# Streamed weight blocks of a recurrent attention layer, copied in DRAM so that a partition's three blocks lie together and are read in longer runs

## Chip, cores and metric

One core of a Trainium2 chip runs the whole kernel in one launch. The metric is the device time of a run in microseconds (us); runs shown here are of the same kernel and input, and the profile is one more execution with the hardware profiler on.

## Reference

Four layers are applied in turn, A, B, A, B, each added to its input. Both A layers use the same weights. The change lies in layer A, whose heart is a recurrence over 64 segments of 32 rows with 8 memory rows ahead of them:

```python
for s in range(n_seg):                       # 2048 / 32 = 64
    xs = x[:, s * seg_len:(s + 1) * seg_len, :]
    h = concatenate([mem, xs], axis=1)       # 8 + 32 rows of 640
    q, k, v = (einsum('btd,dhe->bhte', h, W) for W in (Wq, Wk, Wv))   # 32 heads of 192
    p = softmax(where(mask, einsum('bhqe,bhke->bhqk', q, k) * scale, -1e9))
    o = einsum('bhqk,bhke->bhqe', p, v)
    o = einsum('bhte,hed->btd', o, Wo)       # back to 640
    mem = o[:, :M, :]                        # the next segment waits for this
    outs.append(o[:, M:, :])
```

Layer B is a linear attention over all rows at once; the change does not touch it.

## The kernel before, in words

Each A layer has a part ahead of the recurrence (`A_pre`), which projects the last 8 rows of every segment, and the recurrence itself (`A_chain`). In the chain the 32 heads are worked off in four rounds of eight heads; even segments take the rounds in the order 0, 1, 2, 3 and odd ones in the order 3, 2, 1, 0. A round needs its columns of Wq, Wk and Wv: five blocks each (the 640 input rows are five blocks of 128 partitions) of 1536 bf16 columns, 3072 bytes a partition. The arena in SBUF holds most of these blocks for good (`res`). Three blocks of each matrix, of rounds 0 and 3 alone, share nine slots (`slot`, `SLOTS`), and the 12 row blocks of Wo of rounds 0 and 3 share one buffer (`wo_end`). So in every segment one of the two rounds is overwritten by the other: 9 blocks of 384 KB and 1920 KB of Wo, 5.4 MB, are streamed from DRAM per segment.

The order is written out by hand. In the first round of a segment (`n == 0`) `project` (L988) goes through the blocks with the slots first, and as soon as a slot's block has been multiplied, `load_slot` (L681) issues on SyncE (SP) the load of the same block for the last round of this segment; Q and V blocks in one transfer of 384 KB, K blocks in two of 192 KB, that is in runs of 3072 and 1536 bytes. After the second round's scores, `wo_round` (L1067) multiplies the first round's output with `wo_end`, and `load_wo` (L698) issues six transfers of 320 KB (runs of 2560 bytes out of `wo_rows`, a copy of Wo's rows laid out partition by partition). That makes 18 transfers per segment on SP's queue. The last round reads the Q blocks, the K blocks, the V blocks and at the segment's end all of `wo_end`; then the new memory rows go through VectorE (L1229, L1230) into the next segment's input `hT`, for which its first matmul waits.

GpSimd issues the smaller transfers: `kqb<-kqb` (L959) and `Vp<-vb` (L971) bring the memory rows' parts of Q, K and V for a later round, `otb<-otb` (L1058) stores a tile that has two buffers and is written again by ScalarE (L1053) or VectorE (L1051, L1054), and `Vp<-xn` (L939) brings the next segment's rows. `normalise` (L1115) on VectorE makes the weights `E` for which `attend` (L1038) waits.

`fill` and `SEG_FILL` (L1087) issue weight loads that compute nothing, a few per segment, and `keep_busy` matmuls that compute nothing.

Of the kernel before, what the change touches and what calls it, by code (L numbers as in the profile page):

```python
# [8 lines left out]
P = 128  # L9
BF16 = mybir.dt.bfloat16  # L10
# [7 lines left out]
SLOTS = {"Q": 3, "K": 3, "V": 3}  # L18
# [97 lines left out]
class Kernel:  # L116
# [526 lines left out]
    def layer_A(self, xn_dram, at_dram, li, x_raw=None):  # L643
        nc, tc = self.nc, self.tc
        KC, NSEG = self.KC, self.NSEG
        dram = self.dram
        NR = 4
        PW = 1536
        self.kqb_d = dram.tile([NR, P, NSEG, 192], BF16, name=f"kqb{li}")
        self.vb_d = dram.tile([NSEG, NR, 2, 8, 896], BF16, name=f"vb{li}")  # L650
        self.otb_d = dram.tile([P, NSEG, 384], BF16, name=f"otb{li}")
        wview = self.wview
        wov = self.A_Wo.rearrange("h d m -> (h d) m").rearrange("(c p) m -> p c m", p=P)
        low = self.view(0, LATE)
        at = LATE
        res, slot = {}, {}
        for r in (3, 2):
            for m in "KQV":
                for b in range(KC - (SLOTS[m] if r == 3 else 0)):
                    res[m, r, b] = low[:, len(res) * PW:len(res) * PW + PW]  # L660
        assert len(res) * PW * 2 == LATE
        for m, r, b in [(m, 0, b) for m in "KQV" for b in range(KC - SLOTS[m])] + \
                [(m, None, b) for m in "KQV" for b in range(KC - SLOTS[m], KC)] + [(m, 1, b) for m in "KQV" for b in range(KC)]:
            v = self.view(at, 2 * PW)
            at += 2 * PW
            if r is None:
                slot[m, b] = v
            else:
                res[m, r, b] = v
        holds = {}  # L670
        wo_mid = self.view(at, 24 * 1280)
        wo_end = self.view(at + 24 * 1280, 12 * 1280)
        assert at + 36 * 1280 == ARENA
        unread = set(res)

        def load_slot(m, r, b, whole=False):
            if holds.get((m, b)) != r:
                holds[m, b] = r
                w = PW if whole or m in "QV" else PW // 2
                for h in range(0, PW, w):  # L680
                    nc.sync.dma_start(out=slot[m, b][:, h:h + w], in_=wview[m][:, b, PW * r + h:PW * r + h + w])  # L681

        def load_matrix(m, r):
            for b in range(KC):
                if (m, r, b) in unread:
                    unread.remove((m, r, b))
                    nc.sync.dma_start(out=res[m, r, b], in_=wview[m][:, b, PW * r:PW * r + PW])
                elif (m, r, b) not in res:
                    load_slot(m, r, b, True)

        early = {(0, 4), (0, 5), (2, 4), (2, 5), (1, 0), (1, 1), (1, 2), (1, 3)}

        def load_wo(r, into=None, part=range(6)):
            t = into if into is not None else wo_end[:, :] if r in (0, 3) else wo_mid[:, 7680 * (r - 1):7680 * r]
            for k in part:
                tk = t[:, 1280 * k:1280 * k + 1280]
                if r in (0, 3):
                    self.last_load = nc.sync.dma_start(out=tk, in_=self.wo_rows[r // 3, :, 1280 * k:1280 * k + 1280])  # L698
                else:
                    nc.sync.dma_start(out=tk.rearrange("p (c m) -> p c m", m=640),  # L700
                                      in_=wov[:, 12 * r + 2 * k:12 * r + 2 * k + 2, :])

        def piece(m, r, b):
            assert (m, r, b) in res or holds[m, b] == r
            return res[m, r, b] if (m, r, b) in res else slot[m, b]

        if li == 0:
            self.wo_rows = dram.tile([2, P, 7680], BF16, name="wo_rows")

        def lay_out_wo(i):  # L710
            nc.sync.dma_start(out=self.wo_rows[i].rearrange("p (c m) -> p c m", m=640), in_=wov[:, 36 * i:36 * i + 12, :])

        def early_wo():
            for r in (2, 0, 1):
                load_wo(r, part=[k for k in range(6) if (r, k) in early])

        def late_wo(r, part=range(6)):
            load_wo(r, part=[k for k in part if (r, k) not in early])

        self.A_pre(xn_dram, li, load_matrix, piece, wo_mid, wo_end, lay_out_wo, early_wo, x_raw)  # L720
        self.A_chain(xn_dram, at_dram, li, load_slot, piece, load_wo, late_wo, wo_mid, wo_end, low)
        self.post_args = at_dram, wo_mid, wo_end, low

    def two_heads(self, ap):
# [188 lines left out]
        if x_raw is None:  # L913
            self.small.close()

    def A_chain(self, xn_dram, at_dram, li, load_slot, piece, load_wo, late_wo, wo_mid, wo_end, low):
        nc, tc, KC, NSEG = self.nc, self.tc, self.KC, self.NSEG
        scale = float(self.Dh) ** -0.5
        NR = 4
        with tc.tile_pool(name=f"A{li}_ch", reuse_waits="tile", bufs=1) as sp, \  # L920
# [17 lines left out]
            def load_rows(s):  # L938
                nc.gpsimd.dma_start(out=xr[8:32, :], in_=xn_dram[32 * s:32 * s + 24, :])  # L939

            def hx_transpose(hT, gs):
                for g in gs:
                    nc.vector.transpose(out=hT[32 * g:32 * g + 32, :, :],
                                        in_=xr[:, 160 * g:160 * g + 160].rearrange("p (j b) -> p b j", b=KC))
# [89 lines left out]
            def attend(E, n, OT=None):  # L1034
                O = [pop.tile([P, 512], F32, name=f"ps_o{x}", tag=f"o{x}") for x in range(2)]
                for x in range(2):
                    for k, e, i in ((0, 0, 0), (320, 1, 2), (128, 0, 1), (192, 1, 1)):
                        nc.tensor.matmul(O[x][:, 80 * i:80 * i + 80], lhsT=Vs[n % 2][0:80, 448 * x + k:448 * x + k + 128],  # L1038
                                         rhs=E[0:80, 160 * x + 80 * e:160 * x + 80 * e + 80], start=(k == 0),
                                         stop=(k == 192), skip_group_check=True)  # L1040
                if OT is None:
                    OT = sp.tile([P, 6, 64], BF16, name="OT", tag="OT")
                o = [x[:, 0:240].rearrange("p (i q) -> p i q", q=80) for x in O]
                nc.scalar.activation(out=OT[:, 0:3, :], in_=o[0][:, :, 0:64], func=ACT.Copy)  # L1044
                nc.vector.tensor_copy(out=OT[:, 3:6, :], in_=o[1][:, :, 0:64])
                return OT, o
# [80 lines left out]
            hT = new_hT()  # L1127
            hx_transpose(hT, range(4))
            load_rows(1)
            for s in range(NSEG):  # L1130
                W = pop.tile([P, 512], F32, name="ps_w", tag="w")
                order = rounds(s)
# [4 lines left out]
                def q_or_k(m, n):  # L1137
                    ps = pqp.tile([P, 512], F32, name="ps_qk", tag="qk")
                    project(hT, ps, m, n, s, range(KC))
                    return to_raw(ps, "OT" if m == "K" and n == 0 else "raw")  # L1140
# [4 lines left out]
                def tails_after(n):  # L1145
                    if n + 2 < NR:
                        extra_v(s, n + 2)
                    elif s + 1 < NSEG:
                        extra_v(s + 1, n + 2 - NR)
# [15 lines left out]
                for n in range(L):  # L1165
                    raw = q_or_k("Q", n + 1)
                    if n > 0:
                        OT, o = attend(Ep, n - 1)
                        tails_after(n - 1)
                    S, E = weigh(False)  # L1170
                    to_rows(raw, "Q")
                    if n > 0:
                        otb = keep_tail(o)
                    next_kq(s, n)
                    if n > 0:
                        store_tail(otb, s, order[n - 1])
                    to_rows(q_or_k("K", n + 1), "K")
                    sums(S, E)
                    normalise(S, E)
                    if n == 1:  # L1180
                        wo_round(W, order[n - 1], OT, True, False)
                        if n == 1:
                            if s < NSEG - 1:
                                load_wo(order[L])
                            else:
                                tails = [self.fetch_tails(tb, low) for tb in range(2)]
                    if n + 1 < L:
                        pv = v_banks()
                        project(hT, pv, "V", n + 1, s, range(KC))
                        v_rows(pv, n + 1)  # L1190
                    Ep = E
# [122 lines left out]
```

## Time and profile before

| what | value |
|---|---|
| runs | 3577.23, 3579.53, 3584.39 us; median 3579.53 us |
| the profiled execution's own time | 3596.84 us |
| its span, first to last instruction | 3595.1 us |
| granted TensorE clock, mean | 0.992 |
| PE busy | 3303.2 us (92%) |
| the two chains | about 205.9 to 1515.4 us and 2008.0 to 3318.6 us, 1309.5 and 1310.6 us |
| DMA share in the two chains | 0.83 and 0.83, at 287 and 286 GB/s |

PE is TensorE's matmuls, PEld its weight loads, DVE VectorE, ACT ScalarE, POOL GpSimd, SP SyncE. A wait is a stretch in which an engine stood idle, put down to what ended it; "issue" is a stretch that nothing in the profile's semaphores explains. "DMA share" is the mean busy share of the core's 16 DMA engines. Queue q1 is SP's, q0 GpSimd's, q8 TensorE's instructions.

### The profile page before, as it was taken

The numbers are of one execution on the slowest core, as the hardware profiler recorded it, in microseconds if no ns is written. First come the engines' busy times: TensorE is split into PE (matmuls) and PEld (weight loads), VectorE is DVE, ScalarE is ACT, GpSimd is POOL, SyncE is SP. The second block draws the span as 40 slices with busy tenths as digits, with TensorE's granted clock in tenths as the row PEclk, the third lists the DMA queues.
The fourth block names the chain that finished last, engine by engine and source line by source line (L and its number), as shares of the span: only waits on it lengthen the run. The fifth ranks groups of instructions, "written<-read, shape, count | busy, mean of one in ns | idle before, by whom it ended". The sixth has DMA issues, their size and how long they took to land.

```text
span 3595.1 us, 168452 instructions
## 1 busy us (share of the span) xinstructions
PE 3303.2 (92%) x70978; PEld 2275.7 (63%) x71391; DVE 2332.6 (65%) x6320; ACT 2034.5 (57%) x5233; POOL 1588.9 (44%) x4173
## 2 busy tenths in 40 slices
PE   9989999999999989989999889999999999999899
PEld 7756666666666666655377566666666666666553
DVE  5456666667667766746643566766676666776465
ACT  3356666666666656646432556666666666666463
POOL 3345555555555555530123455555555555555400
PEclk9999999999999999999999999999999999999999
DMA  8888888888888878860476888888888888888600
GB/s 319 325 289 279 287 294 284 277 290 296 282 284 293 296 272 283 297 217 1 145 275 216 289 273 276 292 283 292 274 296 287 290 279 290 299 278 287 221 1 30
DMA packets 452689, 929.38 MB, mean 259 GB/s; under 512 B 75338, under 2 KB 218330, under 8 KB 448858
## 3 DMA queue, kind: packets, MB, share of 16 engines
q1 hardware_dynamic: 382266, 817.56, 64.6%
q0 software_dynamic: 67744, 87.80, 8.0%
q8 instruction: 557, 9.13, 1.0%
q10 hardware_dynamic: 1920, 13.24, 0.9%
q14 instruction: 202, 1.65, 0.1%
HBM read 848.50 MB, written 73.73 MB: 257 GB/s over the span
## 4 chain that ended last, share of the span: by engine, by line
PE 47%; DMA 29%; DVE 9%; issue 6%; ACT 5%; POOL 1%; PEld 1%; SPq 1%; ACTq 0%; DVEq 0%; POOLq 0%
DMA arena<-wo_rows 18%; PE ps_qk L988 14%; PE ps_v L988 5%; DMA arena<-in_A_Wv_dram 5%; PE ps_pre L878 5%; PE ps_w L1067 4%; PE ps_o L1038 3%; PE ps_s L1030 3%; PE ps_pre L902 2%; DVE E L1115 2%; ACT raw L998 2%; DMA Vp<-vb 2%; PE kv L1269 2%; DVE QT L1006 1%; PE ps_s L1025 1%
## 5 line engine op out<-in xcount | busy, mean ns | idle before, releaser
L988 PEld LDWEIGHTS <-hT 128*32 128x32 bf16 x30720 | 874.4, 97 | 418.8 <-DVE hT L1230 53.9
L988 PE MATMUL ps_qk<-arena,hT 128*32 128x384 bf16 x20480 | 1031.0, 327 | 64.0 <-DVE hT L1230 55.8
L998 ACT ACTIVATE raw<-ps_qk 128x384 bf16<-128x384 f32 x1024 | 501.9, 490 | 366.1 <-DVE QT L1008 249.9
L988 PE MATMUL ps_v<-arena,hT 128*32 128x384 bf16 x10240 | 601.7, 327 | 22.8 <-DMA arena<-in_A_Wv_dram 22.3
L1067 PE MATMUL ps_w<-arena,OT 128*32 128x160 bf16 x18432 | 488.3, 234 | 46.4 <-DMA arena<-wo_rows 37.3
L971 POOL DMA_DIRECT2D Vp<-vb x512 | 258.3, 505 | 594.3 <-PE ps_o L1038 561.7
L1067 PEld LDWEIGHTS <-OT 128*32 128x32 bf16 x18432 | 391.0, 96 | 123.4 <-issue 53.8
L1003 DVE STREAM_TRANSPOSE KT<-raw 128x384 bf16<-128x384 bf16 x512 | 296.2, 578 | 195.4 <-ACT raw L998 191.5
L1006 DVE STREAM_TRANSPOSE QT<-raw 128x256 bf16<-128x256 bf16 x512 | 227.9, 445 | 238.5 <-ACT raw L998 196.2
L959 POOL DMA_DIRECT2D kqb<-kqb x512 | 290.9, 568 | 168.6 <-POOL KT L967 147.3
L1058 POOL DMA_DIRECT2D otb<-otb x512 | 282.8, 552 | 149.2 <-DVE otb L1054 117.0
L1019 DVE CAST Vp<-ps_v 64x384 bf16<-64x384 f32 x512 | 286.1, 559 | 85.8 <-ACT Vp L1017 74.5
L1115 DVE TENSOR_TENSOR E<-E,ps_s 80x320 bf16<-80x320 bf16 x512 | 247.4, 483 | 118.0 <-ACT ps_s L1114 117.1
L1017 ACT ACTIVATE Vp<-ps_v 64x384 bf16<-64x384 f32 x512 | 245.2, 479 | 107.6 <-PE ps_v L988 107.2
L1038 PEld LDWEIGHTS <-Vp 80*128 80x128 bf16 x4096 | 193.5, 99 | 175.2 <-issue 140.3
L1038 PE MATMUL ps_o<-E,Vp 80*128 80x80 bf16 x4096 | 233.1, 201 | 71.7 <-DVE E L1115 45.9
L1092 ACT ACTIVATE E<-ps_s 80x320 bf16<-80x320 f32 x512 | 221.4, 432 | 73.2 <-PE ps_s L1030 35.8
L951 ACT ACTIVATE Vp<-ps_w 32x160 bf16<-32x160 f32 x512 | 150.3, 294 | 157.9 <-DVE wt L1229 144.7
L964 POOL COPY QT<-kqb 128x64 bf16<-128x64 bf16 x512 | 124.4, 243 | 255.8 <-PE ps_s L1030 249.4
L1030 PE MATMUL ps_s<-QT,KT 128*80 128x80 bf16 (+1 forms) x3072 | 233.2, 213 | 2.7 <-POOL KT L967 2.6
L1044 ACT ACTIVATE OT<-ps_o 128x192 bf16<-128x192 f32 x384 | 126.1, 328 | 192.8 <-PE ps_o L1038 177.7
L1113 ACT ACTIVATE ps_s<-ps_s 80x320 f32<-80x320 f32 x512 | 214.7, 419 | 26.9 <-PE ps_s L1108 26.9
(158 smaller groups left out, 5362.3 us busy)
## 6 DMA issues: line engine op xcount, KB each, us to landing
arena<-wo_rows SPq DMA_DIRECT2D x780, 320.0 KB, 7.1
arena<-in_A_Wq_dram SPq DMA_DIRECT2D x427, 384.0 KB, 4.6
arena<-in_A_Wv_dram SPq DMA_DIRECT2D x427, 384.0 KB, 6.5
arena<-in_A_Wk_dram SPq DMA_DIRECT2D x768, 192.0 KB, 4.8
kqb<-kqb POOLq DMA_DIRECT2D x512, 48.0 KB, 5.3
arena<-in_A_Wk_dram SPq DMA_DIRECT2D x43, 384.0 KB, 7.7
vb<-arena POOLq DMA_DIRECT2D x128, 112.0 KB, 6.4
Vp<-vb POOLq DMA_DIRECT2D x512, 28.0 KB, 4.8
```

What stands on the lines that cost most here:

```text
L959: nc.gpsimd.dma_start(out=kqb[:], in_=self.kqb_d[r, :, s, :])
L971: nc.gpsimd.dma_start(out=Vs[n % 2][64:80, :], in_=self.vb_d[s, r].rearrange("g t f -> (g t) f"))
L988: nc.tensor.matmul(o[32 * g:32 * g + 32, 0:384], lhsT=hT[:, b, :], rhs=rhs, start=(i == 0), stop=(i == KC - 1), tile_position=(0, 32 * g), ...
L998: nc.scalar.activation(out=raw[:], in_=ps[:, 0:384], func=ACT.Copy)
L1003: nc.vector.transpose(out=KT[:, :, 0:64], in_=raw[:, :].rearrange("p (c j) -> p c j", j=64))
L1006: nc.vector.transpose(out=QT[:, :, 0:4:3, 0:64], in_=rv[:, :, 0:3:2, :])
L1019: nc.vector.tensor_copy(out=o, in_=i)
L1030: nc.tensor.matmul(S[0:80, c0:c0 + 80 * (q1 - q0)], lhsT=KT[:, 3 * x + i, :], rhs=QT[:, x, q0:q1, :], start=False, stop=(x == 1 and i == 2 ...
L1038: nc.tensor.matmul(O[x][:, 80 * i:80 * i + 80], lhsT=Vs[n % 2][0:80, 448 * x + k:448 * x + k + 128], rhs=E[0:80, 160 * x + 80 * e:160 * x ...
L1058: nc.gpsimd.dma_start(out=self.otb_d[:, s, 96 * r:96 * r + 96], in_=otb[:, :, :].rearrange("p c t -> p (c t)"))
L1067: nc.tensor.matmul(W[32 * g:32 * g + 32, 0:160], lhsT=OT[:, c, q:q + 32], rhs=w[:, 640 * i + 160 * g:640 * i + 160 * g + 160], start=(firs ...
L1115: nc.vector.tensor_tensor(out=E[0:80, 0:320], in0=E[0:80, 0:320], in1=rc, op=ALU.mult)
```

## The change

Twelve transfers in the first layer's chain, one per segment (segments 0 to 11), copy the slots' blocks of rounds 0 and 3 from the weights to DRAM tiles in which the three blocks of a partition lie together; half of the partitions (64) at a time, 576 KB. They are issued on SP behind the segment's Wo transfers. From the segment in which both halves of a matrix and round are there, and in all of the second layer A's chain, its slots are loaded from the copy: Q in two transfers (one block, then two: runs of 3072 and 6144 bytes), K and V in one transfer each (runs of 9216 bytes), which are issued when the last of the blocks that they overwrite has been read. Wo comes in three transfers of 960, 640 and 320 KB (runs of 7680, 5120 and 2560 bytes), in every segment of both layers. The bytes that reach SBUF are the same. A segment has 7 transfers on SP's queue in place of 18. The instructions of the other engines stay as they were.

```diff
             v = self.view(at, 2 * PW)
-            at += 2 * PW
             if r is None:
                 slot[m, b] = v
+                slot_at.setdefault(m, at)
             else:
                 res[m, r, b] = v
+            at += 2 * PW
         holds = {}
+        if li == 0:
+            self.together = {(m, r): dram.tile([P, SLOTS[m], PW], BF16, name=f"w{m}{r}")[:] for r in (0, 3) for m in "QKV"}
+            self.copied = {}
+
+        def copy_slots(m, r, half):
+            p = slice(64 * half, 64 * half + 64)
+            nc.sync.dma_start(out=self.together[m, r][p], in_=wview[m][p, KC - SLOTS[m]:KC, PW * r:PW * r + PW])
+            self.copied[m, r] = self.copied.get((m, r), 0) + 1
+
+        def load_slots(m, r, b):
+            first = KC - SLOTS[m]
+            if m == "Q" and b == first:
+                done = (first, first + 1)
+            elif b == KC - 1:
+                done = (first + (m == "Q"), KC)
+            else:
+                return
+            b0, b1 = done
+            if all(holds.get((m, k)) == r for k in range(b0, b1)):
+                return
+            for k in range(b0, b1):
+                holds[m, k] = r
+            nc.sync.dma_start(out=rows[m][:, PW * b0 - PW * first:PW * b1 - PW * first],
+                              in_=self.together[m, r][:, b0 - first:b1 - first, :].rearrange("p b n -> p (b n)"))
+
+        rows = {m: self.view(slot_at[m], 2 * PW * SLOTS[m]) for m in "QKV"}
...
         def load_slot(m, r, b, whole=False):
-            if holds.get((m, b)) != r:
+            if not whole and self.copied.get((m, r)) == 2:
+                load_slots(m, r, b)
+            elif holds.get((m, b)) != r:
                 holds[m, b] = r
                 w = PW if whole or m in "QV" else PW // 2
...
-        def load_wo(r, into=None, part=range(6)):
+        def load_wo(r, into=None, part=None):
+            if part is None:
+                t = into if into is not None else wo_end
+                for k0, k1 in ((0, 3), (3, 5), (5, 6)):
+                    self.last_load = nc.sync.dma_start(out=t[:, 1280 * k0:1280 * k1],
+                                                       in_=self.wo_rows[r // 3, :, 1280 * k0:1280 * k1])
+                return
...
             load_rows(1)
+            copies = [(m, r, half) for m in "QKV" for r in (0, 3) for half in range(2)] if li == 0 else []
             for s in range(NSEG):
...
                             if s < NSEG - 1:
                                 load_wo(order[L])
+                                if copies:
+                                    copy_slots(*copies.pop(0))
```

More of the change, by code (lines that the diff above doesn't have):

```diff
@@ L655, in layer_A @@
         at = LATE
-        res, slot = {}, {}
+        res, slot, slot_at = {}, {}, {}
         for r in (3, 2):
@@ L720, in layer_A @@
         self.A_pre(xn_dram, li, load_matrix, piece, wo_mid, wo_end, lay_out_wo, early_wo, x_raw)
-        self.A_chain(xn_dram, at_dram, li, load_slot, piece, load_wo, late_wo, wo_mid, wo_end, low)
+        self.A_chain(xn_dram, at_dram, li, load_slot, piece, load_wo, late_wo, wo_mid, wo_end, low, copy_slots)
         self.post_args = at_dram, wo_mid, wo_end, low
@@ L914, in A_pre, with A_chain @@
             self.small.close()
-    def A_chain(self, xn_dram, at_dram, li, load_slot, piece, load_wo, late_wo, wo_mid, wo_end, low):
+    def A_chain(self, xn_dram, at_dram, li, load_slot, piece, load_wo, late_wo, wo_mid, wo_end, low, copy_slots):
         nc, tc, KC, NSEG = self.nc, self.tc, self.KC, self.NSEG
```

## The prediction, made before the changed kernel ran

> **What bounds the kernel now.** I read the page first (engine shares, then the queues), then one segment by windows, then the waits of PE, then SP's timeline. From the page:
>
> ```profile
> span 3595.1 us, 168452 instructions
> PE 3303.2 (92%) x70978; PEld 2275.7 (63%) x71391; DVE 2332.6 (65%) x6320; ACT 2034.5 (57%) x5233; POOL 1588.9 (44%) x4173
> q1 hardware_dynamic: 382266, 817.56, 64.6%
> q8 instruction: 557, 9.13, 1.0%
> ```
>
> PE is nearly full, but the loads run close behind. The q8 row matters later: 9.13 MB in 557 packets is 16 KB each, and PE's and PEld's 142,369 instructions make 256 per packet, so TensorE's own program comes through the same 16 DMA engines. Next, the windows of one segment (904.9 to 925.6 us), by stage: the K loads, V and the first of Wo, Wo, and the end.
>
> ```profile
> 909.50:913.50 4.00, 3.68 (x90) 2.64 (x86) 3.03 (x9) 2.87 (x8) 1.79 (x6) 1.00 1.02 339
> 913.50:916.70 3.20, 3.20 (x108) 2.55 (x101) 2.24 (x6) 1.96 (x5) 1.71 (x5) 1.00 1.01 383
> 916.70:920.00 3.30, 3.30 (x84) 2.40 (x82) 2.40 (x8) 2.55 (x8) 2.46 (x7) 1.00 1.03 378
> 922.50:924.70 2.20, 1.56 (x51) 1.10 (x51) 1.77 (x5) 0.54 (x2) 1.60 (x3) 1.00 0.34 96
> ```
>
> The last two columns are the DMA share and GB/s. From 906.2 to 922.5 us the DMA engines are full (share 0.94 to 1.05), then idle for four. The 1536-byte K runs move 339 GB/s, the 3072-byte and 2560-byte ones 383 and 378. What PE waits for:
>
> ```profile
> PE ps_w L1067 <- issue: 39.5, 70, 1.2
> PE ps_w L1067 <- DMA arena<-wo_rows: 37.3, 80, 1.9
> PE ps_v L988 <- DMA arena<-in_A_Wv_dram: 22.3, 32, 3.8
> PE ps_o L1038 <- DMA Vp<-vb: 13.8, 29, 1.2
> ```
>
> Columns: us, times, longest. Asked for the two chains alone, Wo has 32.5 us (11.9 + 20.6) and V 13.0 (5.4 + 7.6). So a segment, 20.85 us on average (126 of them in 2620 us), loses about 0.36 us to the streamed blocks. The first row is not a load of the kernel: it is PE waiting for its own instructions. SP's timeline of the same segment:
>
> ```profile
> 905.26 2.38 SPq L681 DMA_DIRECT2D arena<-in_A_Wq_dram  x3
> 907.74 2.76 SPq L681 DMA_DIRECT2D arena<-in_A_Wk_dram  x6
> 910.59 1.95 SPq L681 DMA_DIRECT2D arena<-in_A_Wv_dram  x3
> 914.12 3.07 SPq L698 DMA_DIRECT2D arena<-wo_rows  x6
> ```
>
> Q, K and V take 7.3 us to issue although PE has freed all slots by 907.5. In the compiled order each transfer waits for the one eight places ahead of it to land, so SP keeps at most eight on their way.
>
> **Longer runs.** The trace's records of single packets give medians of 65 ns for 1536 bytes, 102 for 2560, 121 for 3072, 196 for 5120 and 460 for 12288: 9 ns and 0.0366 ns a byte. By that line 6144, 7680 and 9216 bytes take 233, 290 and 346 ns. Each DMA engine serves eight partitions. Before: 8 x (3x121 + 6x65 + 3x121 + 6x102) = 13.8 us a segment. After: 8 x (121+233 + 346 + 346 + 290+196+102) = 13.1 us. With 11 fewer 9-ns semaphore packets that is 0.85 us less, and Wo lands that much earlier. Its wait is 0.47 us a time (37.3 us, 80 times), so nearly all of the 32.5 us goes, and V's 13.0 with it: minus 45 us. I cost the new grouping at nothing: K and V are issued when their third block has been read, and Q is still in the queue then; V must land whole before its first block is used, 0.33 us sooner than its last one today, out of the 0.85. The first Wo transfer waits for half of `wo_round` instead of a sixth (some 0.4 us later), and V is still in the queue then; without that cover it would cost those 0.4 us a segment. The eleven fewer issues are SP's time, which nobody waits for.
>
> **The copies.** Twelve of 576 KB. Lower price: 12 packets per DMA engine at 121 ns, 1.5 us, inside the idle stretch behind Wo, which holds about 3.3 us of free queue (2.2 x 0.66, 0.9 x 0.86, and 1.3 x 0.84 at the next segment's start): nothing. Upper price: the 1920 KB copy `wo_rows<-in_A_Wo_dram` took 19.9 us to land, so 6.0 us, 2.7 beyond the gap, for 12 segments 32 us. I take 0.8 us each, nearer the gap: plus 10 us. SP waits for a copy only where its second half was issued one segment earlier (round 3), some 9 us before.
>
> **What the earlier issue does to the fetches of instructions.** This decides my forecast. A segment has almost exactly 1024 TensorE instructions, so its four fetches fall at fixed times: asked for when PE starts the block before, 0.9, 6.5, 11.3 and 17.2 us into the segment. From the packet records, their packets start 0.5, 1.8, 3.3 and 1.2 us later (medians), take 1.0 us, and PE goes on at the earliest 1.43 us after their end (1.24 to 1.61 in the 52 longest stalls). PE needs 5.65, 4.75, 5.2 and 4.4 us per block. The third is late today (3.3 + 1.05 + 1.43 = 5.8 against 5.2), and that is the issue row above. The second has 0.59 us to spare (its packet ends 2.02 us before PE needs the block, less the 1.43). It waits behind what SP has issued; at 911.2 us that is little, because the eight-transfer limit holds V back. With one transfer each, K and V both are queued by 908.5, and at 911.2 the queue holds the rest of K (1.2 us) and all of V (2.8).
>
> How long does the fetch then wait? Bounds: 1.8 us as today, and 4.0, all that is queued. Rows between: the third fetch, behind a full queue of 3072 and 2560 bytes, 3.3 us; two fetches at a chain's end with the 12288-byte `otb` loads ahead of them, 4.0 and 3.7. I take 3.3, the nearest full queue. PE then stalls 3.33 - 1.78 - 0.59 = 0.96 us in each segment with both K and V copied: 53 segments of the first chain (from the twelfth on) and 64 of the second, plus 112 us. The third fetch still finds a full Wo queue and I leave it. Nothing hides this stall: it falls ahead of `attend` in the third round, and PE is what that part of the segment runs on.
>
> The Trainium skill would hide it. Its page "Runtime: NRT & Kernel Launch", section "Instruction fetch mechanics", says that instructions come in 16 KiB blocks by the sequencer's own DMA queue, as the q8 row shows here, and that the cost of crossing a block is "mostly hidden"; by that the sum would lack the 112 us. The issue row, 39.5 us in 70 stalls, shows that it is not always so in this kernel.
>
> The sum, against the profiled execution's own 3596.84 us: -45 + 10 + 112 = +77, 3674. That execution was 0.5% above the median of the runs, 3579.53, so by ratio 3656.
>
> **Rivals.**
>
> Faster, the fetch stays in time. The mechanism: the DMA engines take instruction packets in before the queued weights, so that the wait at 6.5 us stays under 2.4 us. For it: with 1536-byte packets the wait is only 1.8 us. Against it: 3.3 to 4.0 us wherever the queue was full or its packets large. Then -45 + 10, 3545; with a free copy 3535. The Trainium skill's "mostly hidden" is this case. Chance 0.27.
>
> A draw: the fetch waits 2.4 to 2.8 us, which costs 0.1 to 0.4 us in 117 segments and cancels the 35. 3565 to 3600. Chance 0.13; of this 0.07 within the bound.
>
> Worse: the fetch waits for all that is queued, 4.0 us, so that the stall is 1.6 us (187 us), and the `otb` store issued in the Wo phase, which lands 5.6 us after issue, lands later than VectorE can bear. Its buffer is written again (L1051) 6.0 us after that issue, with 0.6 us of slack before `E`; 46 such waits, 29.2 us, are there today. 3720 and more. Chance 0.10.
>
> That runs of 9216 bytes are split again by the DMA engines, so that only SP's order changes: speaks against it that 12288-byte packets are in the records whole. It would give the stall without most of the gain, 3690; part of the 0.50 that I give my forecast.
>
> **How the numbers follow.** No change means within 0.2% (7 us), about what three runs of this kernel can tell apart. Faster: 0.27 and the lower 0.02 of the draw. Slower: forecast 0.50, worse 0.10, upper 0.04 of the draw. The forecast's own range is 3610 (stall 0.6 us) to 3700 (1.3). The range 3540 to 3710 reaches to the faster case and leaves out the worse one and half of the faster one's lower side.
>
> **What would show it.** q1's packets fall from 382,266 to about 196,000. Q, K and V are issued within 3 us of a segment's start. The wo_rows wait falls under 10 us, V's under 5. If I am right, the issue rows of PE rise from 40 to some 150 us, with a new stall about 11 us into each segment, and the segment grows to 21.5 us; the first twelve segments of the first chain, whose K and V are not yet copied, get shorter instead. A fetch that starts under 2.4 us after its request in the K phase would make the forecast wrong, and segments of 20.5 us would follow.

## The result, and the profile after

| | before | after |
|---|---|---|
| median of the runs beside each other | 3581.96 us (4 runs) | 3618.65 us (4 runs) |
| ratio after to before | | 1.0102, 95% interval 1.0076 to 1.0128 |
| the profiled execution's own time | 3596.84 us | 3620.12 us |

The changed kernel is 37 us slower; 77 were forecast. The two profiled executions are only 23 us apart, since that of the kernel before lies 15 us above its median. The page of the profile after, in the rows that were shown of before:

```profile
span 3618.4 us, 166133 instructions
PE 3296.9 (91%) x70978; PEld 2277.0 (63%) x71391; DVE 2331.4 (64%) x6320; ACT 2028.7 (56%) x5233; POOL 1596.8 (44%) x4173
q1 hardware_dynamic: 190650, 824.56, 60.0%
q8 instruction: 557, 9.13, 1.0%
```

SP's queue moves the same weights, and 7 MB of copies, with half the packets and 4.6 points less of the DMA engines' time, and PE computes as much as before. So the loads did get cheaper, and the time went somewhere else. Windows of one segment of the first chain (929.5 to 950.8 us), cut by the stages used before; the columns are busy time and instructions of PE, PEld, DVE, ACT and POOL, then clock, DMA share, GB/s:

```profile
934.70:938.70 4.00, 3.68 (x89) 2.65 (x85) 3.03 (x9) 2.87 (x8) 1.78 (x6) 1.00 1.02 408
938.70:941.90 3.20, 3.20 (x107) 2.50 (x99) 2.24 (x6) 1.82 (x5) 1.75 (x6) 1.00 1.05 381
941.90:945.20 3.30, 3.30 (x87) 2.42 (x84) 2.28 (x8) 2.54 (x8) 2.13 (x7) 1.00 0.99 402
945.20:947.70 2.50, 1.50 (x46) 1.13 (x47) 1.84 (x6) 1.77 (x5) 1.60 (x6) 1.00 0.64 239
```

The K stage moves 408 GB/s (339 before), the Wo stage 402 (378). In the last row the queue already runs dry (share 0.64), and yet PE works 1.50 us of 2.50. What PE waited for:

```profile
PE ps_w L1102 <- issue: 106.3, 119, 2.3
PE ps_qk L1023 <- DVE hT L1268: 75.1, 126, 0.7
PE ps_v L1023 <- DMA arena<-wV: 5.4, 2, 4.6
PE ps_o L1073 <- DMA Vp<-vb: 5.4, 4, 2.9
PE ps_w L1102 <- DMA arena<-wo_rows: 4.8, 7, 1.2
PE ps_v L1023 <- DMA arena<-in_A_Wv_dram: 3.5, 3, 2.8
```

Wo went from 37.3 to 4.8 us, V from 22.3 to 8.9 (two rows), `Vp<-vb` from 13.8 to 5.4: 54 us less. The first row, PE waiting for its own instructions, rose by 67 us, the wait for the next segment's memory rows by 19; its row before was

```profile
PE ps_qk L988 <- DVE hT L1230: 55.8, 126, 0.6
```

SP's timeline of that segment, and PE's where it stalls:

```profile
930.49 0.81 SPq L694 DMA_DIRECT2D arena<-wQ  x2
931.63 1.16 SPq L694 DMA_DIRECT2D arena<-wK  x1
932.88 0.38 SPq L694 DMA_DIRECT2D arena<-wV  x1
939.63 1.27 SPq L726 DMA_DIRECT2D arena<-wo_rows  x3
```

```profile
946.52 0.23 PE L1102 MATMUL ps_w<-arena,KT 128*32 128x160 bf16 x1
947.63 1.01 PE L1102 MATMUL ps_w<-arena,KT 128*32 128x160 bf16 x47 [0.88 <-issue]
```

Q, K and V are all queued 3.8 us into the segment. (Times in a segment are counted here and below from some 0.6 us ahead of its first weight load for Q, which stands at 930.1 us.) The stall stands at 17.2 us, in the middle of `wo_round`: that is the block that the third fetch brings, and not, as forecast, a new place at 11 us.

To see this in numbers I set PE's instruction records beside q8's packets. A segment is four blocks of 256 instructions; the border of a block is the first instruction that its fetch brings. For each block I give the mean time PE takes for it, and below it the median wait of the fetch that is asked for at the block's start, from then to the packet's start (second chain, 62 segments, us):

```
               block 1      block 2      block 3      block 4      segment
before         5.66         4.80         5.80         4.91         21.16
  fetch waits  0.53         1.76         3.23         1.33
after          5.66         5.03         6.27         4.40         21.36
  fetch waits  0.55         2.53         3.81         1.14
```

Putting a border one instruction earlier or later moves single values by 0.1 to 0.2 us, so the split between the blocks holds to that. Where PE stalled for over 0.9 us in the changed kernel, it went on 1.2 to 1.6 us after the packet's end (median 1.4). The second block lost 0.23 us, the third 0.47; the fourth won 0.51. Net 0.20 us, times 126 segments 25 us: the 23 us between the two profiled executions.

The packet records also tell what the DMA engines worked off during these waits, in us of each engine's time. For the second fetch it is 1.7 us of K's pieces before, and 2.6 us of K's and V's after. For the third it is 0.9 us of V's and 2.0 of Wo's before, 0.1 and 3.5 after. So for nearly all of their wait these fetches stand behind SP's loads.

### The profile page after: what moved, and what is told of

It is laid out like the page before. It is cut to its first block, busy times and chain, and to the rows that moved or that the text cites. A ratio compares the mean times of both kernels' runs of the same rounds, so it can differ in the third digit from the quotient of the medians.

```text
span 3618.4 us, 166133 instructions
## 1 busy us (share of the span) xinstructions
PE 3296.9 (91%) x70978; PEld 2277.0 (63%) x71391; DVE 2331.4 (64%) x6320; ACT 2028.7 (56%) x5233; POOL 1596.8 (44%) x4173
## 3 DMA queue, kind: packets, MB, share of 16 engines
q1 hardware_dynamic: 190650, 824.56, 60.0%
## 4 chain that ended last, share of the span: by engine, by line
PE 57%; DVE 12%; ACT 10%; issue 9%; DMA 6%; PEld 4%; POOL 1%; SPq 1%; ACTq 0%; DVEq 0%; POOLq 0%
PE ps_qk L1023 15%; PE ps_w L1102 9%; PE ps_v L1023 6%; PE ps_o L1073 5%; PE ps_pre L913 4%; PE ps_s L1065 4%; DVE E L1150 3%; ACT raw L1033 3%; DVE QT L1041 3%; ACT ps_s L1149 3%; PEld L1102 3%; ACT ps_s L1148 2%; DVE QT L1043 2%; PE ps_pre L937 2%; PE ps_s L1060 2%
## 5 line engine op out<-in xcount | busy, mean ns | idle before, releaser
L1023 PE MATMUL ps_qk<-arena,hT 128*32 128x384 bf16 x20480 | 1043.0, 328 | 87.0 <-DVE hT L1268 75.1
L1023 PE MATMUL ps_v<-arena,hT 128*32 128x384 bf16 x10240 | 594.1, 326 | 9.0 <-DMA arena<-wV 5.4
L1102 PE MATMUL ps_w<-arena,OT 128*32 128x160 bf16 x18432 | 466.8, 234 | 12.2 <-DMA arena<-wo_rows 4.8
L1102 PE MATMUL ps_w<-arena,KT 128*32 128x160 bf16 x6144 | 162.9, 238 | 106.4 <-issue 106.3
L1080 DVE CAST OT<-ps_o 128x192 bf16<-128x192 f32 x384 | 137.5, 358 | 161.6 <-PE ps_o L1073 152.0
## 6 DMA issues: line engine op xcount, KB each, us to landing
arena<-wV SPq DMA_DIRECT2D x117, 1152.0 KB, 10.3
```

What stands on the lines that cost most here:

```text
L1023: nc.tensor.matmul(o[32 * g:32 * g + 32, 0:384], lhsT=hT[:, b, :], rhs=rhs, start=(i == 0), stop=(i == KC - 1), tile_position=(0, 32 * g), ...
L1102: nc.tensor.matmul(W[32 * g:32 * g + 32, 0:160], lhsT=OT[:, c, q:q + 32], rhs=w[:, 640 * i + 160 * g:640 * i + 160 * g + 160], start=(firs ...
```

## The experiments

The theory: transfers that have just been queued in great amount make TensorE's fetch of instructions late, and PE pays for it where its block has no time to spare. The rivals: something else that the change adds costs the time (the copies, the long runs, Wo's grouping, what the full queue does to other transfers), and where the fetches fall does not matter. Times are medians; each ratio is an estimate against runs of the kernel before on the same chip, and not the exact quotient of two medians. Waits and blocks are those of the second chain, as in the table above.

**One part at a time: Wo in three transfers alone**, in the kernel before:

```diff
-        def load_wo(r, into=None, part=range(6)):
+        def load_wo(r, into=None, part=None):
+            if part is None:
...
+                for k0, k1 in ((0, 3), (3, 5), (5, 6)):
...
```

> The kernel before with only Wo read in three transfers. The changed kernel's third instruction fetch of a segment (asked for 11.3 us into it) waits 3.8 us in the queue where it waited 3.3, and costs most. Theory, fetches wait behind queued weight work, and the three Wo transfers are what the third fetch meets: its wait rises to about 3.8, 0.5 us x 126 segments = +60 us, less some 20 us of Wo waits: about 3620 us against 3582. Rival, the third fetch is late because Q, K and V are queued sooner: no change or a small gain, 3560 to 3585, third fetch still 3.3.

Measured: 3597.96 us, 1.0044 (1.0026 to 1.0062). The third fetch waits 3.18 us (3.23 before) and its block takes 5.77 (5.80): nothing changed there, and the rise to 3.8 us that was expected is not seen. In its profile Wo is waited for 26.2 us. So Wo's grouping alone does not make the fetch late; it costs a little, and I have no line that shows where.

**Q, K, V grouped, Wo in six as before**, in the changed kernel:

```diff
-        def load_wo(r, into=None, part=None):
-            if part is None:
...
-                return
+        def load_wo(r, into=None, part=range(6)):
```

> The changed kernel with Wo in six transfers of 2560-byte runs as before; Q, K, V copied and in long runs. If the three Wo transfers delay the third fetch: it falls back to 3.3 us, the second stays at 2.5, time 3560 to 3585 us. If the early and long K and V transfers do it: third fetch stays at 3.8, time 3610 to 3625 us.

Measured: 3621.55 us, 1.0109 (1.0082 to 1.0136), the time of the whole change. The second fetch waits 2.51 us, the third 3.59 (block 5.95). The grouping of Q, K and V makes the second fetch later by itself. The third lies between the two waits that were expected, 3.3 and 3.8: somewhat less late than with grouped Wo, and `Vp<-vb` takes that back (18.4 us of wait, 5.4 in the changed kernel).

**The twelve copies alone**, written and never read, in the kernel before:

```diff
...
+                                if copies:
+                                    copy_slots(*copies.pop(0))
...
```

> The kernel before with the twelve copies issued and never read. Both theories: 0 to 32 us, my sum had 10: about 3590. If the copies were the loss, 3610 or more, all of it in the first twelve segments of the first chain; the second chain unchanged at 1311 us.

Measured: 3588.99 us, 1.0003 (0.9986 to 1.0020). The copies cost nothing; 10 us were in my sum.

**Seven transfers with short runs**: Q, K, V in the changed kernel's grouping, from the weights in runs of 3072 bytes, no copies:

```diff
...
-                              in_=self.together[m, r][:, b0 - first:b1 - first, :].rearrange("p b n -> p (b n)"))
...
+                              in_=wview[m][:, b0:b1, PW * r:PW * r + PW])
...
```

> The changed kernel's seven transfers per segment (also in all of the first chain), but Q, K and V read from the weights as they lie, in runs of 3072 bytes, with no copies. Queue-depth theory: the fetches wait as in the changed kernel (second 2.5 us, third 3.8), and the time is that or a little more, 3610 to 3640 us. Rival, packet length: with 3072-byte packets the second fetch waits 1.8 to 2.0 us as before and the time is 3565 to 3585 us plus what Wo's long runs cost.

Measured: 3623.09 us, 1.0117 (1.0087 to 1.0147). The waits of the second and third fetch are 2.64 and 3.72 us, the same as in the changed kernel (2.53, 3.81), and PE's row for instructions is too:

```profile
PE ps_w L1102 <- issue: 101.4, 123, 1.7
```

So the long runs of Q, K and V and their copy neither cause the loss nor, here, bring a gain that is seen. What is left is that a segment has 7 transfers, and when they are issued; the next run parts these two.

**The old 18 transfers, issued where the changed kernel issues them**, with the old lengths of runs and no copies:

```diff
-            nc.sync.dma_start(out=rows[m][:, PW * b0 - PW * first:PW * b1 - PW * first],
...
+            for k in range(b0, b1):
+                for h in range(0, PW, PW // 2) if m == "K" else (0,):
...
+                    nc.sync.dma_start(out=slot[m, k][:, h:h + w], in_=wview[m][:, k, PW * r + h:PW * r + h + w])
...
```

> The old 18 transfers of a segment, with the old sizes and runs, read from the weights, no copies; but those of Q, K and V are issued where the changed kernel issues them, when the last of the blocks that they overwrite has been read. It differs from the kernel before only in these times, and from the grouped kernel with short runs only in the number of transfers. Theory 'number': with eight in flight at most, the queue is as short as before, the second and third fetch wait about 1.8 and 3.2 us, Wo and V are late again: 3580 to 3600. Rival 'issue time': the fetches wait 2.5 and 3.8 us as in the changed kernel: 3610 to 3630.

Measured: 3587.53 us, 1.0009 (0.9989 to 1.0029): the kernel before.

```profile
PE ps_w L1104 <- issue: 46.1, 74, 1.6
PE ps_w L1104 <- DMA arena<-wo_rows: 29.2, 72, 1.2
```

K's six transfers go out from 3.2 to 5.6 us and V's from 6.1 to 7.7, as in the kernel before, although there they are asked for block by block. In the compiled order each transfer waits for the one eight places ahead to land: in the chains of this run and of the kernel before, none goes out earlier than that, and 16 to 19% go out within 0.1 us of it. With 18 small ones this holds V back until about the time when the second fetch is asked for (6.9 us); with 7 large ones it holds nothing back (12 us or more lie between in the run before). So for the time the number of transfers is the cause, and the place in the program is not. The fetches' waits are not wholly those of the kernel before, though: the second waits about 2.0 us and the third 3.5, where the kernel before has 1.76 and 3.23 and the run with seven transfers 2.64 and 3.72. What the third's part of this comes from, no run shows.

**Sixteen transfers with long runs**, the changed kernel's cut by partitions (32 for K and V, 64 for part of Q and Wo):

```diff
...
+            cuts = (0, 128) if b1 - b0 == 1 else (0, 64, 128) if b1 - b0 == 2 else (0, 32, 64, 96, 128)
...
```

> The changed kernel with the same long runs, cut by partitions into 16 transfers for a segment (Q in three, K and V in four each, Wo in five) instead of 7, so that the limit of eight transfers in flight holds SyncE's queue shorter again; the fetch points stay. Theory 'the queue's depth makes the fetches late, not the runs' length': waits of the second and third fetch back near the 1.8 and 3.2 us of the kernel before (2.5 and 3.8 in the changed kernel), waits for Wo and V again 20 to 45 us together; time 3580 to 3600. Rival 'a queued run of 9216 bytes is what the fetch stands behind': waits 2.5 us or more at the second fetch, 3.8 or more at the third, 3615 to 3660.

Measured: 4753.81 us, 1.3270 (1.3238 to 1.3302). Neither theory is tested, since the loads themselves became slow:

```profile
span 4765.7 us, 167432 instructions
q1 hardware_dynamic: 208170, 824.63, 70.5%
```

The bytes are those of the changed kernel, but they take 70.5% of a span that is a third longer; a packet of 9216 bytes takes 679 ns (median) where it takes 347 in the changed kernel.

**The third fetch without the Wo transfers**, the changed kernel with a segment's Wo loads left out:

```diff
                             if s < NSEG - 1:
-                                load_wo(order[L])
                                 if copies:
```

> The changed kernel without the segments' Wo transfers (the first round's rows stay in their buffer, so the last round multiplies with the wrong ones); nothing else is moved. Theory 'the third fetch is late because it is asked for just after the Wo transfers were queued': its wait falls from 3.8 us to under 2.5, the 1.1 us that it costs in each of 124 segments goes, with the 5 us of waits for Wo: 3485 us, 3460 to 3510. The second fetch, asked for before them, keeps its wait of 2.5 us. Rival 'the third block is slow for another reason': 3605 to 3615, the waits for Wo alone.

Measured: 3501.68 us, 0.9758 (0.9722 to 0.9793); 3485 was expected, in 3460 to 3510.

```profile
PE ps_w L1102 <- issue: 2.2, 3, 1.4
PE ps_w L1102 <- DMA arena<-wo_rows: 3.2, 4, 1.2
```

The third fetch waits 1.06 us, its block takes 5.10 (6.27), and the instruction row is gone; the second fetch, asked for before Wo, waits 2.58 as ever and its block takes 5.02. So fetch 3 is late because of the Wo transfers that are queued 0.9 to 1.8 us ahead of it.

**Moving the fetch points.** `FILL` issues weight loads that compute nothing, once in the first segment. 64, 128 or 192 more of them shift all later block borders by that many instructions and touch no load. In the changed kernel:

```diff
-FILL = {0: 78, 2: 79}
+FILL = {0: 78 + 64, 2: 79}
```

> The changed kernel with 64 more of the weight loads that compute nothing, once, in the first segment of the first layer: every later point at which TensorE has used up 256 instructions and asks for the next block falls 64 instructions earlier in its segment. Loads, copies and their order are those of the changed kernel. Theory 'fetch': the four points move from 1.2, 6.9, 11.8 and 18.1 us of a segment to about 5.6, 10.4, 16.1 and 20.2 us. Between them lie 4.8, 5.8, 3.6 to 4.2 and 6.4 us of TensorE's work, and a block costs nothing if its wait stays 2.43 us below that. The waits read from the changed kernel by their time in the segment (0.55, 2.5, 3.8 and 1.15 us) make about 2.0, 3.4, 2.0 and 0.6 us at the new points, so only the third is late, by about 0.9 us, in place of 0.2 and 1.1 us: 0.4 us less on each of 124 segments, near 3570 us where the changed kernel takes 3620; between 3545 and 3600. Rival 'depth': long transfers of a full queue slow the chain by what else they delay (GpSimd's transfers, the weights themselves): the position of the fetches does not matter, 3620 within 6.

> As the run before with 128 more loads instead of 64. Theory 'fetch': the points fall at about 4.2, 9.7, 14.4 and 19.2 us with 5.5, 4.7, 4.8 and 6 us of work between them; waits of about 1.7, 3.2, 2.7 and 0.9 us there make the second late by 1.0 and the third by 0.3 us, 1.3 us in a segment, the same as in the changed kernel: near 3620 us, 3590 to 3650. Rival 'depth': 3620 within 6. The two are told apart by which fetch is late, not by the time.

> As the two before with 192 more loads. Theory 'fetch': the points fall at about 2.5, 9.2, 13.3 and 17.4 us with 6.7, 4.1, 4.4 and 5.6 us of work between them; waits of about 1.0, 3.1, 3.2 and 1.5 us make the second late by 1.4 and the third by 1.2 us, 2.6 us in a segment where the changed kernel has 1.3: 160 us more, near 3780, and above 3680 in any case. Rival 'depth': 3620 within 6.

and in the kernel before:

> The kernel before, with 64 more of the weight loads that compute nothing, once, in the first segment, as in the run of the changed kernel that became 3704 us. Theory 'fetch': the old order of loads is sensitive to the place of the fetch points too, since it also keeps up to eight transfers queued; at the new points (5.6, 10.4, 16.1 and 20.2 us) the work of the third block is only 3.6 to 4.2 us, so at least 0.5 us of a segment is lost there: 3640 us, and not below 3600. Rival 'only the grouped queue makes fetches late': 3582 within 10.

> The kernel before with 128 more such loads. Theory 'fetch': the points are those of the changed kernel's run of 3642 us; there the second fetch, in front of the Wo loads, waited only 1.5 us and the first was late behind the just issued K and V. The old order issues K and V block by block, so the first should be less late: 3570 to 3620, 3595. Rival 'only the grouped queue': 3582 within 10.

Measured (ratio to the kernel before as it was; the last column is the one ratio by the other, with the two intervals' half widths added as squares):

```
borders moved by   changed kernel                    kernel before                     change by itself
0                  3618.65 1.0102 (1.0076-1.0128)    1                                 1.010 (1.008-1.013)
64                 3704.50 1.0349 (1.0328-1.0370)    3677.05 1.0253 (1.0219-1.0286)    1.009 (1.005-1.013)
128                3641.82 1.0172 (1.0150-1.0194)    3716.67 1.0362 (1.0323-1.0402)    0.982 (0.977-0.986)
192                3725.21 1.0414 (1.0376-1.0451)    not tried
```

A few instructions that compute nothing, once, cost up to 132 us in the kernel before. The theory that the fetches are late holds, and the rival that their place does not matter is out. And the change itself is 1% slower at two places and 1.8% faster at a third. The instruction rows of the changed kernel moved by 192, and of the kernel before moved by 128:

```profile
PE ps_w L1102 <- issue: 182.4, 125, 3.0
```

```profile
PE ps_w L1067 <- issue: 186.2, 246, 2.0
```

My times for the changed kernel were wrong for 64 (a gain was expected, and it lost 2.4%), near for 128, and too high for 192. For 128 that was luck: the second fetch was to be late, and it waited only 1.5 us; the late one was the first, which waited 3.7. In the kernel before, both times were too low (3640 and 3595 expected, 3677 and 3717 measured). I had drawn a straight line between four measured waits. Put together, the waits in the changed order are a saw:

```
asked at, us    1.2   2.5   4.3   5.6   6.9   9.0   10.3   10.9   11.8   14.0   15.0   17.6 and later
waits, us       0.6   1.4   3.7   3.1   2.5   2.5   1.5    4.1    3.8    2.9    2.7    1.1
```

They jump when K and V (2.1 and 2.9 to 3.3 us) or Wo (10.1 to 11.0; 10.6 to 11.5 in the run with the point at 10.3) have just been queued, and fall on the whole as that load drains. A fetch is late if its wait and 2.4 us more (1.0 for the packet, 1.4 until PE goes on) are longer than PE's work in the block before.

**16 instructions more**, a small move towards what looked like more cover:

> The changed kernel with 16 more of the loads that compute nothing, once: the fetch points at about 0.9, 6.5, 11.3 and 16.9 us, with 5.6, 4.8, 5.4 and 4.6 us of work between them. Theory 'fetch', with the waits read at 6.9 and 11.8 us kept: the third has 0.2 us more cover, so 20 to 30 us less than the changed kernel: 3595. Rival: the waits rise by as much as the points move towards the issue of the loads (0.5 us earlier, nearer to 10.1 us): 3620 to 3640.

Measured: 3632.12 us, 1.0119 (1.0096 to 1.0142). The rival of that expectation: the third fetch, asked 0.1 us earlier, waits 3.85 us, and its block takes 6.35. No gain.

**Wo behind the third fetch.** One of the weight loads at a segment's end is moved and reads the Wo buffer, so that the Wo transfers (in the changed kernel with the copy behind them) can only follow it; a segment's instructions stay 1024. First at the start of the third `attend`, in the changed kernel:

```diff
-SEG_FILL = 2
+SEG_FILL = 1
...
+                    if n == 2:
+                        nc.tensor.ldweights(wo_end[:, 0:1])
+                        if s < NSEG - 1:
+                            load_wo(order[L])
...
```

> The changed kernel; one of the two weight loads that compute nothing at a segment's end is moved to the start of the third attend (12.1 us of a segment) and reads the Wo buffer, and the three Wo transfers stand behind it, so SyncE can issue them about 2 us later, just after TensorE has asked for its third block (11.8 us) instead of just before. Instructions per segment and their places stay. Theory 'place': the third fetch's wait falls from 3.8 us towards the 1.06 us of the run without Wo, which takes 1.1 us off the segment; in return Wo lands later: 1920 KB behind what is left of V take about 6.5 us from 12.2 us, to 18.7 to 19.5 us, where the last round needs them at 18.6 us once the third stall is gone, and the fourth fetch (16.9 us) now falls among them. Both together 0.2 to 0.9 us: 3501 + 25 to 110 us, 3560, and below the kernel before's 3585. Rival 'the load has to be paid in any order': at least 3605.

Then behind the third round's scores, and the first of these moves in the kernel before:

> As the run before, with that load and the Wo transfers behind the third round's scores, about 0.8 us later (12.9 us). Theory 'place': the third fetch's wait is 1.1 us, the last Wo lands 0.8 us later than in the run before: 3500 + 60 to 180 us, 3610, slower than the run before by 30 to 100 us if Wo is what is late there. Rival 'the load has to be paid in any order': at least 3605 and the same as the run before within 10.

> The same move in the kernel before: its 18 transfers, Wo in six, issued behind the third attend's start. There the third fetch waits 3.3 us and costs 0.6 us of a segment, and Wo was already late by 37 us in all. Theory 'place': the third wait falls below 2.5 us, 0.6 us times 124 = 75 us less, and Wo is late by about 1 us more: 3585 + 0 to 90 us; 3620. Rival 'the load has to be paid in any order': 3585 within 10.

and at two places between, ahead of the last round's Q and behind two of its five blocks:

> The changed kernel with the Wo transfers behind the weight load that reads their buffer, as in the run that issued them at 12.7 to 13.5 us, but with that load in front of the last round's Q instead of behind it, 1.1 us earlier: issue at about 11.6 us, the third fetch is asked for at 11.8 us, so little of Wo is queued ahead of it. Theory 'a place between exists': the third fetch waits under 2.7 us and costs under 0.3 us of a segment where the changed kernel loses 1.1; Wo and Vp are waited for 20 to 30 us in all instead of 72; 3550 to 3590, 3570. Rival 'every place pays': the third fetch still waits 3 us or more, or the waits come back elsewhere, 3605 to 3630.

> As the run before with that load behind the second of the five blocks of the last round's Q, some 0.3 us later. Theory 'a place between exists': the third fetch waits 1.1 to 2 us and costs nothing, Wo and Vp are waited for 30 to 50 us; 3565 to 3600, 3580. Rival 'every place pays': 3605 to 3630.

Measured (first Wo issue and third fetch by their medians; the third is asked for at 11.8 to 12.1 us, 12.0 to 13.0 where the segment has become long; counted from the first weight load for Q instead, Wo goes out at 9.5, 10.8, 11.1, 11.9, 13.7 and 11.8 us and the third fetch is asked for at 11.2 to 11.5, 12.4 behind the scores):

```
                     Wo issued at   fetch 3 waits   block 3   block 4   time     ratio
changed kernel       10.1           3.81            6.27      4.40      3618.65  1.0102 (1.0076-1.0128)
ahead of Q           11.3           4.01            6.30      4.72      3672.05  1.0227 (1.0200-1.0254)
within Q             11.7           3.59            5.86      4.75      3643.56  1.0163 (1.0140-1.0186)
third attend         12.4           1.08            5.09      5.23      3617.74  1.0076 (1.0053-1.0099)
behind the scores    13.9           1.11            5.07      6.72      3797.75  1.0579 (1.0534-1.0625)
before, third attend 13.1           1.01            5.11      6.44      3785.71  1.0477 (1.0433-1.0522)
```

Where Wo goes out behind the fetch, the fetch waits 1.1 us: that part held. The gain did not: all five times were expected too low, by 58 to 188 us. PE's waits with Wo at the third `attend`:

```profile
PE ps_w L1102 <- DMA arena<-wo_rows: 38.2, 94, 1.4
PE ps_o L1073 <- DMA Vp<-vb: 34.1, 77, 1.9
```

Most of the 1.2 us that the third block wins come back (a segment of the second chain takes 21.21 us, 21.36 in the changed kernel): Wo is late again, the memory rows' `Vp<-vb` stands behind it, the fourth fetch now waits 2.22 us (1.14), and the first eleven segments, still with the old loads of Q, K and V, take 22.3 us each in place of 21.5. Earlier places leave the fetch behind Wo. Behind the scores PE waits longer for Wo:

```profile
PE 3392.6 (89%) x70816; PEld 2317.6 (61%) x71391; DVE 2324.3 (61%) x6320; ACT 2037.9 (54%) x5233; POOL 1590.4 (42%) x4173
PE ps_w L1102 <- DMA arena<-wo_rows: 184.3, 249, 2.1
```

That is not all that was lost there. TensorE's granted clock was 0.962 in that profile (0.991 in the changed kernel), and PE is busy for 3392.6 us where it was for 3296.9: about 96 us of the loss are slower matmuls. The kernel before with Wo at the third `attend` has the same (0.958, and 3403.8 us after 3303.2). Why the clock was lower, no run shows. Of the five places none beats the kernel before. The theory that a good place exists between is refuted for those tried.

## Why the prediction was right in direction and wrong in size

- *Packets and loads.* As forecast. Packets of 6144, 7680 and 9216 bytes take 234, 291 and 347 ns (233, 290 and 346 worked out); q1 has 190,650 packets (about 196,000); Q, K and V are issued within 3 us (V, the last, 2.8 us after the first weight load for Q); Wo's wait falls under 10 us. V's is 8.9 us, not under 5.
- *Minus 45 for Wo and V.* The mechanism was right. The fourth block, with the waits for Wo, won 0.51 us, 63 us in 124 segments. Without any Wo loads it takes 4.64 us, 0.27 less than before or 33 us; the other 0.24 of the 0.51 come with the late third block. My reading is that what PE else waits for at the segment's end has arrived by then; no run separates this.
- *Plus 10 for the copies.* Measured on their own they cost nothing. The lower bound was the right one.
- *Plus 112 for the second fetch.* The mis-sized term. Its wait rose from 1.76 to 2.53 us, not to 3.33, and past the 0.59 us to spare that left 0.23 us a segment, 29 us. I had taken the third fetch as a measure of a full queue. By the packet records some 197 pieces of K and V were still queued when the second was asked for, close to what I had reckoned, but only some 116 of them were started ahead of it: K's rest and 48 of V's 128. My reading is that it counts how long ago the load was queued: Wo went out 0.9 to 1.8 us ahead of the third fetch, V and K 3.6 and 4.8 us ahead of the second, and asked at 4.3 us, 1.4 us behind V, a fetch does wait 3.7. That is not the whole, for with Wo in three alone Wo goes out at the same times as in the changed kernel, and the third fetch waits 3.18 us and not 3.81.
- *The third fetch left at nothing.* The step that failed outright. "The third fetch still finds a full Wo queue and I leave it" took the wait as already at its most; it rose from 3.23 to 3.81 us, and as that block had nothing to spare, nearly all of it was paid: 0.47 us a segment, 58 us, the largest loss. Hence also the stall at 17 us and not at 11. Most of the rise comes with the grouping of Q, K and V (3.59 us with Wo in six, 3.18 with Wo in three alone): V is then nearly through when the third fetch is asked for, and 3.5 us of Wo's pieces go ahead of it in place of 2.0. Why more of Wo goes ahead then stays open.
- *The sum.* -63 + 29 + 58 = +24 by the blocks, where -45 + 10 + 112 = +77 stood. The direction came from the right cause, the fetches, but on the wrong one of them; two errors partly cancelled, and to that extent it was luck.
- *The other signs.* The first segments did not get shorter (the twelve behind the very first take 257.6 us after 256.2). The instruction row rose to 106.3 us, not 150, and the segment to 21.36 us, not 21.5. That looks nearer than it was: the 20.85 us that the prediction gives for a segment before takes 2620 us for 126 segments. They are 124, of 21.1 us each, so a segment grew by 0.20 us only.

The two rivals on the fast side needed the second fetch in time, or nearly. It was nearly in time (2.53 us, inside the draw's 2.4 to 2.8), and with the third unmoved the sum would have been a draw, -33 + 29. On the rule behind the fast rival, the row first: PE's instruction stalls are 39.5 us before, 106.3 after, up to 186.2 with the borders moved, and 2.2 without Wo. The Trainium skill, "Runtime: NRT & Kernel Launch", section "Instruction fetch mechanics", calls the crossing of a block "mostly hidden". The run without Wo agrees; in the others these rows are what is not hidden. The Trainium skill, "DMA: Bandwidth & Descriptors", section "Queues, rings and completion order", lets an engine go on to its next queue after a packet of typically 9 to 17 descriptors. For the third fetch of the kernel before, the wait by that would be 0.9 to 1.7 us (9 to 17 times the 102 ns of Wo's pieces, an estimate from that page's figure). It was 3.2 us, in which each DMA engine started some 24 pieces of SP's queue, 7 of V's and 17 of Wo's. In the changed kernel the second fetch stands behind some 7 pieces of 347 ns each. The measured waits decide.

## What to carry to other kernels

Where weights stream close to the DMA engines' limit, an engine's own instructions are one more load with a due time: put its block borders (every 256 instructions) on the segment's time axis beside the times at which big loads are queued, and cost any merging or earlier issue of loads by which fetch then stands behind a load that has just been queued. A measured gain or loss of a per cent may be one of place: repeat old and new with the borders moved before a change is called good or bad, as here the sign turned. Fewer, larger transfers lift a limit on the number in flight, and that limit may have been what kept a queue short for others.

## What the hardware showed that was not expected

- A fetch asked for 0.5 us *after* the first Wo transfer was issued waits as long (4.01 us, issue at 11.3) as one asked for behind all three (3.81). At 11.7 the waits of single segments spread from 0.74 to 4.14 us (10th and 90th percentile), at 12.4 they are 1.1: the step lies within 1 us.
- In transfers that cover only 32 or 64 of the 128 partitions the same runs took 1.6 to 2 times as long: 9216 bytes 679 ns for 347, 7680 542 for 291, 6144 376 for 234. Cutting a load by partitions, as a way to have more and smaller transfers, cost 32%. The cause is open: Wo's runs of 2560 bytes, in one whole transfer queued behind cut ones, also took 179 ns for 102, while Q's whole transfer of 3072 bytes kept its 121.
- 64 to 192 weight loads of 79 ns each, issued once, so 5 to 15 us of work, moved the whole kernel's time by 23 to 132 us, their own work included.
